# Slack behind DMA landings for scores and for VectorE and ScalarE steps in a recorded instruction order, and one store moved to another queue

## The chip, the cores and the metric

One core of one Trainium2 chip. The metric is the device time of one execution in microseconds (us).

A ratio "to before" is the mean time of one kernel's runs over the mean of the other's runs of the same rounds, on the same chip, with a 95% interval. It is not quite the ratio of the medians that are quoted beside it.

## The reference

Two layers, each an attention with a compressive memory (segments of 512 tokens, 32 heads of 20) and a feed-forward block, on 2048 tokens of width 640. Cut to what matters:

```python
for s in range(N):                       # N = 4 segments of L = 512
    logits = einsum('bhqd,bhkd->bhqk', qs, ks) * scale + mask
    p = softmax(logits, axis=-1)         # scores, exponentials
    a_dot = einsum('bhqk,bhkd->bhqd', p, vs)
    a_mem = einsum('bhld,bhde->bhle', phi(qs), M) / (phi(qs) @ z + 1e-06)
    o = g * a_mem + (1.0 - g) * a_dot
    M = M + einsum('bhld,bhle->bhde', phi(ks), vs)     # memory, for the next segment
    z = z + sum_l phi(ks)
x = x + o @ wo
x = x + relu(layernorm(x) @ w1) @ w2     # then the same two blocks once more
```

## The kernel before: what the change touches

The program is not written in the order in which it runs. Some forty generators each yield the operations of one job (scores, exponentials, division, feed-forward, stores). A list scheduler, at build time, keeps a predicted clock for each engine and a predicted time for every semaphore value. It picks one operation after another and appends it to that engine's list, and the chip then runs each list in that order. I call this scheduler the recorder.

The choice is made by a key, of which the first entry is the predicted start plus a penalty:

```python
# Sched.run, cut
if isinstance(st[2], Op):
    heads.append((st[0], n, st, self._alts(st[2]), st[2], self._late(st[2])))
elif isinstance(st[2], Either):                       # score steps
    both, lone = st[2].fn()
    if both is not None:
        heads.append((st[0], n, st, self._alts(both), both, 0.0))      # no penalty
...
key = (round(start + late), 0.5 if op.urgent else prio, self.rank[id(st[1])], n)
if best is None or key < best[0]:
    best = (key, st, end, start, k, op)
```

The penalty existed only for TensorE. From the event SOFT_FROM on, an operation whose input has only just become ready is ranked as if it started later, by 400 ns where the input comes from an engine and by 1000 ns where it is a DMA that has to land:

```python
SOFT, SOFT_DMA, SOFT_FROM = 400, 1000, ("sc",6,4,1)    # the original has a line each

def _late(self, op):
    late = 0.0
    if op.alts[0][0] == "pe" and SOFT_FROM in self.events:
        ...
        for t in waits:
            k = (id(t[0]), t[1])
            late = max(late, self.t[k] + SEM_NS + PE_MARGIN + (SOFT_DMA if k in self.landed else SOFT) - start)
    if not op.lag or self.mode != "full":
        return late
    ...
```

The penalty moves no predicted time. It only lets other work go first. The predicted landing of a transpose is made here:

```python
tk = yield dma("sp", slot_sem, 32768 * n, lambda e: e.dma_start_transpose(dst, src), waits,
               issue=max(1400.0, 140.0 * n), lat=2400.0, rate=270.0, holds=True)
```

The VectorE step that is the first one of the division, a reciprocal that waits for a transposed buffer, otk:

```python
w = yield Need("otk", m)              # the transpose's landing
...
tr = yield dve(192, 1, lambda e: e.reciprocal(
    rv, tt.ap.rearrange("p b (h e) -> p b h e", h=4)[:, :, :, DH]), w + rd.tks)
```

The softmax here doesn't subtract the row's maximum and nothing guards it: scores larger than these inputs give would overflow.

## Time and profile before

559.84 us in the median of three runs (558.67 to 560.89).

| from the page and the views | before |
|---|---|
| span of the profiled execution | 556.5 us |
| TensorE busy / VectorE busy / ScalarE busy | 545.8 / 416.2 / 405.5 us |
| TensorE idle from 105.9 to 478.0 us | 2.54 us |
| VectorE's waits for otk, all of the span | 4.2 us in 5 |
| changes of matmul kind after 105.9 us | 263 |

The event of SOFT_FROM falls at 105.9 us, at score matmul 224 of 1024. The prediction says 264 changes of kind; it counted to the end of the span, the table to the last scores. TensorE's timeline shows one of the six gaps (columns: start, length, what, and in brackets the idle time just before and what ended it):

```profile
145.85 0.39 PE L1177 MATMUL ps<-pad 20*128 20x512 bf16 x4
146.67 0.85 PE L658 MATMUL ps<-wo_r,oT 128*128 128x320 bf16 x5 [0.43 <-DVE x_sb L1393]
```

The score matmuls are followed by nothing for 0.43 us, and the release came from VectorE's residual add.

### The profile page before, as it was taken

What the parts mean: (1) busy time and instruction counts of PE and PEld (TensorE: products, weight loads), DVE (VectorE), ACT (ScalarE), POOL (GpSimd) and SP (SyncE); (2) the same over time, 40 slices, a digit from 0 to 9 for tenths busy, and PEclk for the clock granted to TensorE, in tenths of its full rate; (3) what the DMA queues carried; (4) which work ended last, traced back from release to release, by engine and by line L of the source; (5) the groups of instructions that cost most, each with busy time, mean ns of one, the idle gap of its engine ahead of it and who ended that gap; (6) DMA issues with size and microseconds to landing.
All of it is one profiled execution on the core that took longest, in us unless ns stands there. A gap on an engine that the chain in (4) does not pass through costs nothing.

```text
span 556.5 us, 18928 instructions
## 1 busy us (share of the span) xinstructions
PE 545.8 (98%) x8265; PEld 308.0 (55%) x8265; DVE 416.2 (75%) x1063; ACT 405.5 (73%) x514; POOL 192.1 (35%) x302
## 2 busy tenths in 40 slices
PE   8999999999999999999999999999999999999997
PEld 7554554455454555646456554465555654666756
DVE  5967889888899898897778988889965767335102
ACT  5699889899677887798788887887765787432140
POOL 5346344333444244343433443335411433201000
PEclk9999999999999999999999999999999999999999
DMA  8695899844584158274284424872427412333101
GB/s 271 142 231 160 206 192 220 228 60 88 97 172 92 21 105 185 49 113 77 58 203 83 91 45 114 155 122 21 67 59 175 105 44 30 85 83 62 40 2 51
DMA packets 130292, 61.32 MB, mean 110 GB/s; under 512 B 109090, under 2 KB 120098, under 8 KB 130210
## 3 DMA queue, kind: packets, MB, share of 16 engines
q1 hardware_dynamic: 129792, 59.62, 49.7%
q8 instruction: 65, 1.06, 0.8%
q10 hardware_dynamic: 418, 0.49, 0.3%
q14 instruction: 17, 0.14, 0.1%
HBM read 20.57 MB, written 12.85 MB: 60 GB/s over the span
## 4 chain that ended last, share of the span: by engine, by line
PE 83%; DVE 7%; DMA 5%; ACT 2%; SPq 2%; issue 1%; POOL 0%; ACTq 0%; POOLq 0%
PE ps L658 39%; PE ps L661 24%; PE ps L1177 8%; PE ps L1271 6%; DMA otk<-otu 3%; ACT PT L1239 2%; PE ps L1057 1%; PE ps L1114 1%; DMA pad<-scr 1%; PE ps L1310 1%; PE ps L635 1%; PE ps L1451 1%; DVE o_sb L1365 1%; DVE xn_tok L725 1%; SPq L993 1%; DMA scr<-w_r 1%
## 5 line engine op out<-in xcount | busy, mean ns | idle before, releaser
L1239 ACT ACTIVATE PT<-ps 128x1024 bf16<-128x1024 f32 x320 | 309.0, 1028 | 65.9 <-PE ps L1177 61.5
L1251 POOL TENSOR_SCALAR_AFFINE_SELECT PT<-PT 128x512 bf16<-128x512 bf16 x256 | 166.3, 668 | 265.4 <-ACT PT L1239 265.3
L658 PE MATMUL ps<-w_r,hT 128*128 128x320 bf16 x508 | 81.5, 299 | 0.0
L1497 DVE TENSOR_TENSOR x_sb<-x_sb,ps 128x320 bf16<-128x320 bf16 (+1 forms) x65 | 30.8, 474 | 55.3 <-PE ps L661 45.7
L661 PE MATMUL ps<-xnT,w_r 128*32 128x512 bf16 x1144 | 68.3, 379 | 0.3 <-issue 0.3
L1177 PE MATMUL ps<-pad 20*128 20x512 bf16 (+3 forms) x1024 | 63.4, 301 | 3.0 <-ACT PT L1239 2.1
L658 PEld LDWEIGHTS ps<-w_r,hT 128*128 128x128 bf16 x508 | 47.4, 98 | 23.6 <-issue 5.3
L679 DVE BATCH_NORM_STATS2 stats<-x_sb 128x6 f32<-128x320 bf16 x124 | 55.6, 470 | 2.9 <-DMA x_sb<-in_A_x_dram 2.5
L658 PE MATMUL ps<-xnT,w_r 128*128 128x512 bf16 x234 | 57.7, 380 | 0.0
L1476 ACT ACTIVATE hT<-ps 128x512 bf16<-128x512 f32 x57 | 34.1, 599 | 22.0 <-PE ps L661 20.7
L661 PE MATMUL ps<-w_r,hT 128*32 128x320 bf16 (+1 forms) x1348 | 49.7, 294 | 0.0
L1177 PEld LDWEIGHTS ps<-pad 20*128 20x128 bf16 x1024 | 17.9, 92 | 54.7 <-ACT PT L1239 24.5
L661 PEld LDWEIGHTS ps<-xnT,w_r 128*32 128x32 bf16 x1144 | 29.5, 97 | 24.8 <-issue 0.5
L1281 DVE CAST otu<-ps 128x512 bf16<-128x512 f32 x51 | 34.9, 684 | 10.9 <-PE ps L1271 10.8
L1271 PE MATMUL ps<-PT,v_aug 128*21 128x128 bf16 (+3 forms) x896 | 40.5, 301 | 0.0
L661 PEld LDWEIGHTS ps<-w_r,hT 128*32 128x32 bf16 x1348 | 34.6, 97 | 8.9
L1393 DVE TENSOR_TENSOR x_sb<-x_sb,ps 128x320 bf16<-128x320 bf16 x64 | 30.0, 477 | 11.8 <-PE ps L661 8.6
L1475 DVE TENSOR_SCALAR hT<-ps 128x512 bf16<-128x512 f32 x47 | 32.2, 685 | 7.2 <-PE ps L658 5.5
L695 POOL TENSOR_TENSOR rstd<-lnU,mhalf 128x2 f32<-128x2 f32 (+2 forms) x26 | 20.6, 792 | 45.1 <-DVE lnU L691 35.7
L658 PE MATMUL ps<-wo_r,oT 128*128 128x320 bf16 x223 | 35.4, 300 | 0.4 <-DVE x_sb L1393 0.4
L658 PEld LDWEIGHTS ps<-xnT,w_r 128*128 128x128 bf16 x234 | 20.9, 97 | 23.7 <-issue 4.3
L1022 ACT ACTIVATE stg<-stg 128x512 bf16<-128x512 bf16 x50 | 31.5, 634 | 2.5 <-DVE rtmp L1020 2.2
(109 smaller groups left out, 737.8 us busy)
## 6 DMA issues: line engine op xcount, KB each, us to landing
pad<-scr SPq DMA_DIRECT2D x124, 80.0 KB
scr<-stg SPq DMA_DIRECT2D x34, 256.0 KB, 3.5
out_dram<-x_sb SPq DMA_DIRECT2D x15, 160.0 KB, 1.8
w_r<-in_B_w_dram SPq DMA_DIRECT2D x10, 216.0 KB, 2.4
w_r<-in_B_w_dram SPq DMA_DIRECT2D x13, 160.0 KB, 2.9
x_sb<-in_A_x_dram SPq DMA_DIRECT2D x10, 160.0 KB, 3.2
scr<-w_r SPq DMA_DIRECT2D x5, 256.0 KB, 3.2
wv_r<-in_A_wv_dram SPq DMA_DIRECT2D x1, 800.0 KB, 9.0
```

Of the source, the lines that this page charges most:

```text
L658: return e.matmul(view(dst.ap, b), a, b, start=(k == 0), stop=(k == last))
L661: return e.matmul(view(dst.ap[rows], b), part, b, start=(k == 0), stop=(k == last))
L679: tk = yield dve(320, 1, lambda e, c2=c2: e.bn_stats(stats6[:, t % 12, c2, :], x_sb[:, t, c2 * 320:(c2 + 1) * 320]), xt)
L1022: te = yield act(512, lambda e, q=q: e.activation(q, q, ACT.Exp), [tr] + p, psum=False)
L1177: fns.append([(lambda e, z=z, j=j, hh=hh, N=N, o=o, sl=sl, q=hh % 2: e.matmul(slot.ap[:, q, o:o + N], sl.ap[32 * hh:32 * hh + DH, z, 0, 12 ...
L1239: tx = yield act(1024, lambda e, dst=dst, src=src: e.activation(dst, src, ACT.Exp, scale=SCALE), sc + pw)
L1251: tm = yield pool(600.0, lambda e, reg=reg: e.affine_select(out=reg, in_=reg, pattern=[[0, 4], [1, 128]], compare_op=ALU.is_ge, fill=0.0, ...
L1271: fns.append((lambda e, OD, j=j, hh=hh: e.matmul(OD.ap[32 * hh:32 * hh + DH + 1, 128 * j:L], VAUG[vx(a, s)][:, j, 4 * g + hh, :], pt.ap[:, ...
L1281: te = yield evac(L, 1, lambda e: e.tensor_copy(dst, OD.ap), lambda e: e.activation(dst, OD.ap, ACT.Copy), [tk] + OTU[0].tks)
L1475: th = yield evac(512, 1, lambda e: e.tensor_scalar(hT[:, dc, :], bk.ap[:, :], 0.0, None, ALU.max), lambda e: e.activation(hT[:, dc, :], b ...
L1476: lambda e: e.activation(hT[:, dc, :], bk.ap[:, :], ACT.Relu), [tk] + HT.tks)
L1497: ta = yield dve(n, 1, lambda e: e.tensor_tensor(x_sb[:, t, c0:c0 + n], x_sb[:, t, c0:c0 + n], bk.ap[:, 0:n], ALU.add), [tk], urgent=True)
```

## The change

The intent: landings come earlier or later than the recorder thinks, and each engine's list runs in order, so a step that waits for a landing should not stand at the head of a list just when the landing is due. The same slack that TensorE operations have is given to score steps and to steps of the other engines. The last quarter of the output is also issued from ScalarE's queue in place of SyncE's.

```diff
+    def _landing(self, op):
+        start = max([self.free["pe"]] + [self.at(t) + SEM_NS + PE_MARGIN for t in op.waits])
+        soft = SOFT_DMA if SOFT_FROM in self.events else 0.0
+        return max([0.0] + [self.at(t) + SEM_NS + PE_MARGIN + soft - start for t in op.waits
+                           if (id(t[0]), t[1]) in self.landed])
+
     def _late(self, op):
 ...
+        if op.alts[0][0] != "pe" and op.dma is None and SOFT_FROM in self.events:
+            start = max([self.free[op.alts[0][0]]] + [self.at(t) + SEM_NS for t in op.waits])
+            late = max([0.0] + [self.at(t) + SEM_NS + 1000 - start for t in op.waits if (id(t[0]), t[1]) in self.landed])
         if not op.lag or self.mode != "full":
             return late
 ...
-                        heads.append((st[0], n, st, self._alts(both), both, 0.0))
+                        heads.append((st[0], n, st, self._alts(both), both, self._landing(both)))
 ...
-                        S.last = yield dma("sp", dout, 256 * n, lambda e, c0=c0, n=n: e.dma_start(
+                        S.last = yield dma(("sp", "sp", "act")[hf], dout, 256 * n, lambda e, c0=c0, n=n: e.dma_start(
```

## The prediction

> **What bounds the kernel now.** I read the page first, then the busy time by stretch, then the waits of TensorE, and last the chain of waits around TensorE's few gaps. The first line of the page says which engine sets the time:
>
> ```profile
> span 556.5 us, 18928 instructions
> ...
> PE 545.8 (98%) x8265; PEld 308.0 (55%) x8265; DVE 416.2 (75%) x1063; ACT 405.5 (73%) x514; POOL 192.1 (35%) x302
> ```
>
> TensorE is busy for 545.8 us of 556.5, VectorE and ScalarE for three quarters. So an idle microsecond of VectorE or ScalarE costs nothing by itself; it costs only where TensorE then stands still. The program is recorded ahead of time by a list scheduler in the source: it picks the order of each engine's instructions from predicted times, and the chip runs each engine's list in that order. The change touches that order, and only after the event ("sc",6,4,1), the last scores of the seventh pair of head groups. A pair has 32 score matmuls (1024 for 32 pairs), so this is score matmul 224, which starts 105.9 us into the span. The other end is 478.3 us, the last score matmul. What TensorE does in the two stretches after that event:
>
> ```profile
> core 0: us, PE busy (x) PEld busy (x) DVE busy (x) ACT busy (x) POOL busy (x), PEclk, DMA share, GB/s
> 105.90:478.00 372.10, 369.56 (x5139) 200.15 (x5131) 308.65 (x774) 298.15 (x362) 142.77 (x217) 1.00 0.48 97
> 478.00:553.60 75.60, 75.55 (x1865) 50.98 (x1854) 22.33 (x55) 18.83 (x31) 3.06 (x5) 1.00 0.20 47
> ```
>
> Each line is length, then busy time by engine. Over the 372.10 us that the new order can change, TensorE is idle 372.10 - 369.56 = 2.54 us; over the last 75.60 us, 0.05 us. The granted clock is 1.00. The view of waits of TensorE over the same stretch names what ended those 2.5 us:
>
> ```profile
> PE ps L1177 <- ACT PT L1239: 1.3, 2, 0.7
> PE ps L1177 <- DMA pad<-scr: 0.5, 1, 0.5
> PE ps L658 <- DVE x_sb L1393: 0.4, 1, 0.4
> PE ps L658 <- DVE v_aug L912: 0.2, 1, 0.2
> ```
>
> Columns are us in total, times, longest. Only one wait is for a landing directly: scores (L1177) waiting 0.5 us for their pad buffer. The others are waits for ScalarE and VectorE, and the chain that ended last shows what stood behind them. Before the gap at 146.67 us, where the output projection waited for a residual add (x_sb L1393) to free its bank:
>
> ```profile
> 140.31 5.01 DMA otk<-otu
> 145.32 0.02 issue
> 145.34 0.35 DVE rden L1357
> 145.69 0.07 DVE mv L681
> 145.76 0.46 DVE rden L1360
> 146.22 0.79 DVE x_sb L1393 x2
> ```
>
> Columns are start, length, what. VectorE's own timeline shows the mechanism:
>
> ```profile
> 145.34 0.35 DVE L1357 RECIPROCAL rden<-otk 128x32 f32<-128x32 bf16 x1 [1.01 <-DMA otk<-otu]
> ```
>
> VectorE stood 1.01 us in front of a reciprocal whose transposed input had not landed; the scheduler had expected it about then. Everything recorded behind it, the residual adds too, came a microsecond late, and TensorE lost 0.43 us at 146.67 us. The same view for the whole kernel gives "DVE rden L1357 <- DMA otk<-otu: 4.2, 5, 1.0": five such waits, 4.2 us of VectorE. Another (1.04 us, at 189.7 us) stands at the head of the chain into the gap of 0.63 us at 194.9 us, and a third (0.68 us, at 415.3 us) at the head of the chain into the gap of 0.46 us before the last segment's first scores at 425.1 us. In that one the pad landing itself came last.
>
> **What the Trainium skill says.** "PSUM — Partial Sum Buffer", section "Engine vs sequencer instructions": the queues of ScalarE, VectorE and GpSimd are strictly first in, first out. The trace agrees: 1.01 us of idle VectorE at 144.3 us, then adds that did not need the landing. So the recording order alone decides whether a late landing blocks unrelated work. "TensorEngine Tiling (Array Packing)", section "Key Properties": changing the tiling mode drains TensorE. The trace agrees, and gives the price: a 512-column matmul over all 128 rows is followed after a median 216 ns by one of its own kind (439 pairs) but after 312 ns by a score matmul on 20 rows (48 pairs), so some 96 ns a change. I count 264 changes of kind after 105.9 us, 264 x 0.096 = 25 us. "DMA: Bandwidth & Descriptors", section "Issuing engines are not separate DMA queues": issuing from several engines runs on the same 16 DMA engines and saves only the sequencer's issue time. This matters for the last part of the change, below.
>
> **The change part by part.**
> No instruction is added or removed, apart from one store that moves to another queue. Up to 105.9 us the order should be the same: all three new terms are zero until the event is recorded.
>
> Scores. A score step whose pad landed less than 1 us ago (predicted) now yields to other TensorE work. It can concern only the first scores of a pair; 25 of the 32 pairs come after the event, and with four pad buffers most were loaded long before. The trace has one gap of this kind after 105.9 us: 0.46 to 0.53 us at 425.1 us. Worth up to 0.5 us if other work is there to fill it; at 422 to 425 us TensorE was already running output projection for lack of scores, so I count half, 0.25 us.
>
> VectorE and ScalarE. Any step that waits for a landing now ranks as if it could start 1 us after it. These are the reciprocals of the division (L1357), the feature-map steps that wait for the spill to memory (L1020, L1022), and the copies into a buffer which a transpose has just left (L1281). Idle VectorE time in front of landings after 105.9 us is 4.2 (transposes) + 0.5 (spills) = 4.7 us. I expect most of it to go, but VectorE has 308.65 of 372.10 us busy, so it is worth only the TensorE gaps behind it: 0.43 at 146.67 us, some 0.31 (hidden in the modelled ends, 310 ns over the usual start-to-start distance) at 151.8 us, 0.63 at 194.9 us: 1.4 us. The slack has a cost too: the division, and with it the transposes of o and the next loads, may be recorded up to 1 us later. I choose new gaps of 0.6 us in sum.
>
> Sum of gaps: -0.25 - 1.4 + 0.6 = -1.05 us. A floor: even all 2.5 us of gaps together are 0.45% of 559.84.
>
> Changes of kind. A new order also changes how often TensorE goes between score mode and the others. Nothing in the change aims at it; the four-column-group form of the projections lets the scheduler avoid some. I allow 15 changes more or fewer of 264, 15 x 0.096 = 1.4 us either way, with a mean of zero.
>
> The last quarter's store from ScalarE's queue. The group view of that store:
>
> ```profile
> L1525 SPq DMA_DIRECT2D out_dram<-x_sb x3: 332/333/1025, 552.2 to 553.9; - x3
> ```
>
> Three stores, durations minimum/median/maximum. The third starts at 553.95 us, right after its add ends (553.60 + 0.32 = 553.92), and the one before it started at 552.98 and took 0.33, so the queue was free 0.6 us earlier. There is no issue wait to remove. The odd 1025 ns of the third issue lies under its own flight: issue to landing was 2.1/2.2/2.9 us for the three, and the third took 2.2. With the same 16 DMA engines underneath, I expect -0.1 us, the chance of overtaking the slow second store.
>
> Together -1.05 - 0.1 = -1.15; with a little more weight on the good side, as the slack does remove the very waits seen, I take 558.4 us, that is 1.4 us or 0.26% off 559.84.
>
> **The rivals.**
> One: the order is hidden anyway. TensorE is at 369.56 of 372.10 us, and the gaps come back elsewhere because each is 0.3 to 0.7 us, the size of the scheduler's error. Then the result is 559.2 to 560.3, nothing to be seen beside the 558.67 to 560.89 of the three runs. For it: the gaps are few and each has another cause at its end. Against it: three of the four largest have a late landing in their chain.
> Two: changes of kind dominate. If pushed-back scores are grouped better with other four-group work, 20 to 30 fewer changes make -2 to -3 us, 556.5 to 557.5; if scores are split off more, +2 us, 561.5. Nothing in the profile tells which.
> Three: the slack starves the score pipeline at the segment starts. ScalarE already waits 56.5 us for scores after 105.9 us; six segment starts later by 1 us each would be 6 us if TensorE had nothing else. Against it: in the last 75.60 us TensorE runs only feed-forward work with 0.05 us idle, so late scores mostly exchange places with it. I would expect at most 2 us, 561 us.
>
> **Range and chances.** Gaps can give back at most 2.5 us, changes of kind some 1.4 us either way, the tail 0.3 us, and the median of few runs moves by about 1 us. From 558.4 this gives 555.8 to 560.9 for 8 in 10. Two per cent is 11.2 us, over four times the gaps there are; it would take over a hundred fewer changes of kind. So faster by over 2%: 0.02; slower by over 2%: 0.02, for a schedule that goes wrong at a segment start; within 2%: 0.96.
>
> **What would show it.** The new profile should show the same start of the score matmuls up to 105.9 us; TensorE idle of about 1.5 us between 105.9 us and the last scores in place of 2.54; VectorE waits for otk under 1.5 us in place of 4.2; changes of kind within 15 of 264; the third quarter's store issued by ScalarE, landing 2.1 to 2.3 us later. It would be wrong if TensorE's busy time itself moved by over 2 us (changes of kind), if new gaps of over 1 us stood at segment starts, or if the store from ScalarE's queue were issued late or flew longer.

## The result and the profile after

556.49 us in the median of four runs (556.20 to 557.13), against 560.37 us before (558.67 to 561.07). The ratio is 0.9937 with an interval of 0.9911 to 0.9962: 0.6% faster, within 2%. The predicted 558.4 us missed the median by 1.9 us; the range of 555.8 to 560.9 us holds it.

The page of the changed kernel:

```profile
span 554.8 us, 18665 instructions
...
PE 545.8 (98%) x8130; PEld 309.3 (56%) x8130; DVE 412.2 (74%) x1061; ACT 407.3 (73%) x516; POOL 190.0 (34%) x302
```

TensorE's busy time is the same to the tenth, 545.8 us; what went is idle time. The recorder itself had planned the changed order 0.45 us longer (TensorE's end at 547.99 us against 547.54): the plan got longer and the execution shorter. (The planned ends quoted in this document come from running the scheduler of each kernel, not from a trace.) (The counts of matmuls differ because some records are missing from each trace.) The same two stretches as in the prediction, their common end being the last score matmul, now at 476.4 us:

```profile
core 0: us, PE busy (x) PEld busy (x) DVE busy (x) ACT busy (x) POOL busy (x), PEclk, DMA share, GB/s
105.90:476.40 370.50, 369.38 (x5010) 200.93 (x5011) 306.60 (x776) 300.09 (x364) 141.19 (x217) 1.00 0.48 98
476.40:552.00 75.60, 75.26 (x1854) 50.86 (x1846) 22.25 (x55) 18.82 (x31) 2.78 (x5) 1.00 0.24 47
```

TensorE is idle 370.50 - 369.38 = 1.12 us in place of 2.54. The view of its waits over that time has two lines left in place of four:

```profile
PE ps L667 <- DVE hT L1484: 0.9, 1, 0.9
PE ps L1186 <- ACT PT L1248: 0.2, 1, 0.2
```

Line numbers are nine higher in the changed kernel (L1357 is now L1366, L1393 is L1402). At the place of the gap shown above there is none. VectorE's timeline there:

```profile
145.65 1.44 DVE L1402 TENSOR_TENSOR x_sb<-x_sb,ps 128x320 bf16<-128x320 bf16 x3 [0.77 <-PE ps L667]
147.31 0.35 DVE L1366 RECIPROCAL rden<-otk 128x32 f32<-128x32 bf16 x1 [0.22 <-DMA otk<-otu]
```

Three residual adds now run ahead of the reciprocal, which itself waits 0.22 us where it had waited 1.01. VectorE still idles 0.77 us, but in front of an add whose matmul was not done, and TensorE shows no gap there.

The one large gap that is left, 0.86 us at 107.4 us, has the old shape. The chain of waits into it:

```profile
99.72 5.55 DMA otk<-otu
105.27 0.02 issue
105.29 0.35 DVE rden L1366
...
106.73 0.61 DVE hT L1484
107.34 0.05 issue
107.39 0.82 PE ps L667 x3
```

A comparison of the two traces shows that VectorE's first 254 instructions, up to 115.8 us in the trace of before, are the same in both kernels, and TensorE's list up to score matmul 248. So at 107 us both kernels run the same order. The kernel before did not show this gap in its profile, and another run of the changed order (below) did not either. The transpose simply landed later in this execution.

This can be counted, and it is the cleanest evidence in the record. Twelve of the fourteen profiles in this document run the same order here (early_5 and compute_slack, below, do not). In all twelve this transpose of otk is issued 6.3 us before the score matmul of the event. In seven (before, dve_act_only, no_store, store_only, landing_early, all_but_divide, landing_late) it landed 4.26 to 5.04 us after its issue, VectorE waited at most 0.51 us for it, and TensorE shows no gap. In five (the change, scores_only, divide_only, slack_300, slack_2000) it took 5.40 to 5.85 us, VectorE waited 0.86 to 1.32 us, and TensorE then stood still for 0.68 to 0.86 us. The order is fixed, only the landing moves, and the gap comes and goes with it.

### The profile page after: what moved, and what is told of

Read it like the earlier page. It is cut to its first block, busy times and chain, and to the rows that moved or that the text cites. A ratio compares the mean times of both kernels' runs of the same rounds, so it can differ in the third digit from the quotient of the medians.

```text
span 554.8 us, 18665 instructions
## 1 busy us (share of the span) xinstructions
PE 545.8 (98%) x8130; PEld 309.3 (56%) x8130; DVE 412.2 (74%) x1061; ACT 407.3 (73%) x516; POOL 190.0 (34%) x302
## 3 DMA queue, kind: packets, MB, share of 16 engines
q8 instruction: 64, 1.05, 0.8%
## 4 chain that ended last, share of the span: by engine, by line
PE 93%; ACT 2%; DVE 2%; DMA 2%; SPq 0%; issue 0%; POOL 0%; ACTq 0%; POOLq 0%
PE ps L667 45%; PE ps L670 26%; PE ps L1186 9%; PE ps L1280 6%; ACT PT L1248 2%; PE ps L1319 1%; PE ps L1066 1%; PE ps L1123 1%; PE ps L644 1%; DMA otk<-otu 1%; PE ps L1460 1%; DMA beta_bc<-in_A_beta_dram 1%; SPq L982 0%; ACT stg L867 0%; PE ps L758 0%
## 5 line engine op out<-in xcount | busy, mean ns | idle before, releaser
L1260 POOL TENSOR_SCALAR_AFFINE_SELECT PT<-PT 128x512 bf16<-128x512 bf16 x256 | 164.2, 659 | 264.4 <-ACT PT L1248 264.3
L670 PE MATMUL ps<-xnT,w_r 128*32 128x512 bf16 x1112 | 65.4, 379 | 0.2 <-issue 0.2
L667 PE MATMUL ps<-xnT,w_r 128*128 128x512 bf16 x242 | 59.9, 380 | 0.9 <-DVE hT L1484 0.9
L1402 DVE TENSOR_TENSOR x_sb<-x_sb,ps 128x320 bf16<-128x320 bf16 x64 | 30.0, 479 | 18.2 <-PE ps L667 10.3
L667 PE MATMUL ps<-wo_r,oT 128*128 128x320 bf16 x242 | 38.9, 300 | 0.0
L1290 DVE CAST otu<-ps 128x512 bf16<-128x512 f32 x48 | 32.7, 682 | 6.9 <-PE ps L1280 6.3
L866 DVE CAST stg<-ps 128x512 bf16<-128x512 f32 x45 | 30.6, 684 | 5.8 <-PE ps L667 5.6
```

Of the source, the lines that this page charges most:

```text
L667: return e.matmul(view(dst.ap, b), a, b, start=(k == 0), stop=(k == last))
L670: return e.matmul(view(dst.ap[rows], b), part, b, start=(k == 0), stop=(k == last))
L866: te = yield evac(N, 1, lambda e: e.tensor_copy(sg.ap[:, t0:t0 + N], bk.ap[:, 0:N]), lambda e: e.activation(sg.ap[:, t0:t0 + N], bk.ap[:, ...
L1260: tm = yield pool(600.0, lambda e, reg=reg: e.affine_select(out=reg, in_=reg, pattern=[[0, 4], [1, 128]], compare_op=ALU.is_ge, fill=0.0, ...
L1290: te = yield evac(L, 1, lambda e: e.tensor_copy(dst, OD.ap), lambda e: e.activation(dst, OD.ap, ACT.Copy), [tk] + OTU[0].tks)
```

## The experiments

Twelve kernels ran, in three calls of four, each call on one chip with 11 runs of the kernel before beside it and 6 runs of each kernel (5 rounds and the profiled one). All gave correct results. "Idle" is TensorE's idle time from the event to the last score matmul in the profiled execution. "Event to end" is the time from the event to TensorE's last matmul in it; it leaves out what happened before the order differs.

| kernel | ratio to before | interval | median, us | idle, us | event to end, us |
|---|---|---|---|---|---|
| before (profile of the first runs) | 1 | | 560.37 | 2.54 | 447.7 |
| the change | 0.9937 | 0.9911 to 0.9962 | 556.49 | 1.12 | 445.7 |
| scores_only | 0.9991 | 0.9961 to 1.0021 | 558.93 | 1.72 | 448.1 |
| dve_act_only | 0.9959 | 0.9936 to 0.9981 | 557.38 | 0.68 | 445.9 |
| no_store | 0.9939 | 0.9916 to 0.9961 | 556.23 | 0.88 | 445.5 |
| store_only | 0.9995 | 0.9973 to 1.0017 | 559.51 | 3.27 | 448.7 |
| divide_only | 0.9960 | 0.9937 to 0.9982 | 557.49 | 1.75 | 447.1 |
| landing_early | 1.0078 | 1.0048 to 1.0108 | 563.74 | 5.79 | 453.2 |
| compute_slack | 0.9976 | 0.9950 to 1.0002 | 558.35 | 2.55 | 447.8 |
| slack_300 | 0.9974 | 0.9949 to 1.0000 | 558.20 | 1.55 | 446.3 |
| all_but_divide | 0.9977 | 0.9954 to 1.0000 | 557.59 | 0.89 | 446.5 |
| early_5 | 0.9964 | 0.9945 to 0.9984 | 556.92 | 1.01 | 445.6 |
| slack_2000 | 0.9997 | 0.9969 to 1.0025 | 559.15 | 2.14 | 447.5 |
| landing_late | 1.0100 | 1.0075 to 1.0126 | 564.46 | 7.34 | 454.1 |

The medians of before in the three calls were 559.68, 559.46 and 558.80 us, so compare by ratio and not by median across calls.

### The parts alone: scores_only, dve_act_only, no_store, store_only

My theory: the gain is TensorE gaps behind landings that block VectorE's list, so the slack on VectorE and ScalarE carries it. The rivals: the scores' placement carries it; the store does; any new order does.

scores_only: `_landing` and its use alone.

```diff
-                        heads.append((st[0], n, st, self._alts(both), both, 0.0))
+                        heads.append((st[0], n, st, self._alts(both), both, self._landing(both)))
```

> Only the scores' slack behind pad landings (the store stays on SyncE's queue). My theory, that the gain is TensorE gaps behind landings which block an in-order VectorE: this part removes at most the gap of 0.46 us at the last segment's first scores, ratio to before 0.998 to 1.001. Rival (the gain comes from scores that are placed better): ratio 0.995 or lower and most of the whole change's 0.9937. Rival (any new order is worth about this much): anything from 0.993 to 1.004.

Measured: 0.9991, not to be told from 1. TensorE's order is the same as before up to score matmul 788. The gap of 0.46 us at the last segment's first scores (425.1 us before) is gone, as was expected of this part. VectorE's waits for otk rose from 4.2 to 12.5 us, 6.2 us of them in one wait, and the time did not: here such waits cost nothing by themselves.

dve_act_only: the three lines in `_late` alone.

```diff
+        if op.alts[0][0] != "pe" and op.dma is None and SOFT_FROM in self.events:
+            start = ...
+            late = max([0.0] + [self.at(t) + SEM_NS + 1000 - start for t in op.waits if (id(t[0]), t[1]) in self.landed])
```

> Only the slack behind landings for VectorE, ScalarE and GpSimd steps. My theory: most of the gain is here, ratio to before 0.994 to 0.997, VectorE's waits for the transposed otk fall from 4.2 us to under 2.5 us, TensorE idle from the event to the last scores falls from 2.54 to under 1.5 us. Rival (scores are what counts): ratio 0.999 to 1.001.

Measured: 0.9959, idle 0.68 us, VectorE's waits for otk 0.4 us in all. This part gains by itself, and its point estimate is some two thirds of the whole.

no_store: both slack parts, the store as before.

```diff
-                        S.last = yield dma(("sp", "sp", "act")[hf], dout, 256 * n, ...
+                        S.last = yield dma("sp", dout, 256 * n, ...
```

> Both slack parts, last quarter's store still on SyncE's queue. My theory: the store is worth nothing (0.0 +- 0.2 us), so the ratio is the whole change's 0.9937 within 0.001. Rival (the store's queue counts): 0.995 or higher.

Measured: 0.9939, the whole gain. With 0.88 us idle and no gap near 107 us it is also a second look at the changed order. Against dve_act_only its mean is 1.0 us lower, give or take about as much, so on top of the other slack the scores' slack may be worth more than it is alone. Part of this may be changes of kind: dve_act_only has about five more, some 0.5 us at the prediction's 96 ns each (an estimate).

store_only: the one line of the store alone, on the kernel before.

```diff
-                        S.last = yield dma("sp", dout, 256 * n, ...
+                        S.last = yield dma(("sp", "sp", "act")[hf], dout, 256 * n, ...
```

> Only the last quarter's store on ScalarE's queue; the order of TensorE, VectorE and GpSimd is the same as before instruction by instruction. My theory: ratio 0.9995 to 1.0005, the third store issues 0.03 us after its add as before and lands 2.1 to 2.3 us later. Rival: it issues or lands 0.3 us or more earlier, ratio 0.999 or lower.

Measured: 0.9995. The lists of TensorE, VectorE and GpSimd are the same as before, row by row. The store's group view:

```profile
L1525 SPq DMA_DIRECT2D out_dram<-x_sb x2: 332/332/332, 554.0 to 554.8; - x2
L1525 ACTq DMA_DIRECT2D out_dram<-x_sb x1: 368/368/368, 555.8 to 555.8; - x1
```

The third store took 368 ns to issue from ScalarE's queue. From SyncE's it had taken 1025 ns in the profile of before, but its data flew 2.19 us then and 2.31 us here. Nor is 1025 ns the price of SyncE's queue: the same store took 332 or 333 ns from it in scores_only, divide_only, compute_slack and all_but_divide, each time with a flight of 1.5 us. The time that ends the span is the flight. Over the profiled executions it was either near 2.2 us or near 1.5 us from either queue: 1.50 us from SyncE's in divide_only, 1.53 us from ScalarE's in early_5. The move is worth nothing that these runs can see.

This run is also a second look at the order of before, and here lies the size that the prediction missed. The order is the same, the idle time is 3.27 us and not 2.54. TensorE's timeline has a gap which the first profile did not have at all:

```profile
165.06 0.30 PE L658 MATMUL ps<-w_r,hR 128*128 128x320 bf16 x1
166.07 1.89 PE L658 MATMUL ps<-xnT,w_r 128*128 128x512 bf16 x8 [0.71 <-DMA xnT<-xn_tok]
```

In the profile of before the matmuls of the same place ran back to back (164.24 and 164.37 us). I compared the 86 transposes of the two executions one by one, from issue to landing: they differ by 0.16 us on the mean, seven by more than 0.5 us, and the largest difference is 0.98 us. So the same list meets landings that move by up to a microsecond, and which gap opens changes from run to run.

### Which step, and is it the landing: divide_only, all_but_divide, landing_early, compute_slack

divide_only: the slack applies to the division's first reciprocal alone. (In this and the next control the diff is shown against the change's line; the edit was made on the kernel before, without the scores' slack and the store, and also marks the reciprocal with `divides`.)

```diff
-        if op.alts[0][0] != "pe" and op.dma is None and SOFT_FROM in self.events:
+        if getattr(op, "divides", False) and SOFT_FROM in self.events:
```

> Slack of 1 us for one step of VectorE only: the reciprocal that waits for the transposed otk (28 of them). My theory, that late transposes in front of this in-order reciprocal are the main cause: ratio to before 0.994 to 0.997, as with the slack on all VectorE and ScalarE steps (0.9959), VectorE's waits for otk under 1 us. Rival (feature-map steps and copies count as much): ratio 0.998 or higher.

Measured: 0.9960, the same as the slack on every VectorE, ScalarE and GpSimd step. VectorE's waits for otk fell to 1.3 us, not under the 1 us that was expected, but all of it lies before the event.

all_but_divide: every such step but that one.

```diff
-        if op.alts[0][0] != "pe" and op.dma is None and SOFT_FROM in self.events:
+        if op.alts[0][0] != "pe" and op.dma is None and SOFT_FROM in self.events and not getattr(op, "divides", False):
```

> Slack of 1 us for VectorE, ScalarE and GpSimd steps behind landings, but not for the division's reciprocal. My theory: the reciprocal carries the gain, so this is worth nothing, ratio to before 0.998 to 1.001, VectorE's waits for otk 3 us or more. Rival (any one of the parts moves the order to the better): 0.997 or lower.

Measured: 0.9977, with waits for otk of 6.7 us. The expectation of 0.998 or more missed narrowly, and the interval of 0.9954 to 1.0000 reaches both to divide_only's value and to nothing. So divide_only shows that slack on the reciprocal is enough for about two thirds of the gain (by the point estimates); that the rest of the steps are worth nothing is not shown. The profiles do not separate the two kernels either: all_but_divide idles 0.89 us and takes 446.5 us from event to end, divide_only 1.75 and 447.1 us.

The recorder's own model separates them clearly. I replayed each recorded list with the model's durations and let every transpose from the event on land 1 us later than planned. TensorE's end then moves from 547.54 to 559.00 us for before, from 547.58 to 558.51 us for all_but_divide, but only from 548.56 to 549.69 us for divide_only and from 547.99 to 549.59 us for the change. This is the plan and not the chip, where landings move by less and not all together. It shows what the slack buys: an order that late transposes hardly lengthen, and slack on the one reciprocal is enough for that.

landing_early: no slack, but a recorder that expects transposes 1 us earlier from the event on.

```diff
-                           issue=max(1400.0, 140.0 * n), lat=2400.0, rate=270.0, holds=True)
+                           issue=max(1400.0, 140.0 * n), lat=1400.0 if SOFT_FROM in S.events else 2400.0, rate=270.0, holds=True)
```

> No slack anywhere; instead the recorder believes, from the same event on, that every transpose lands 1 us earlier than before. This doubles the suspected cost. My theory: VectorE's waits for otk grow from 4.2 us to 12 us or more, more TensorE gaps stand behind them, ratio to before 1.004 or higher. Rival (the gain of the change is luck of a new order): ratio anywhere from 0.994 to 1.004 with no relation to the waits.

Measured: 1.0078. The recorder's own predicted end of TensorE hardly moved (547.77 us against 547.54), but that is a plan in which transposes land 1 us earlier. Replayed with the landings that before's recorder expects, the same order ends at 559.13 us, so by plan it is 11.6 us worse. On the chip VectorE's waits for otk grew to 15.1 us in 13, TensorE's idle time to 5.79 us. The largest gap shows all links at once; first VectorE's line, then TensorE's two, both from the timeline of landing_early:

```profile
419.86 0.35 DVE L1357 RECIPROCAL rden<-otk 128x32 f32<-128x32 bf16 x1 [2.94 <-DMA otk<-otu]
```

```profile
431.98 0.31 PE L661 MATMUL ps<-w_r,hT 128*32 128x320 bf16 x4
435.22 0.60 PE L1177 MATMUL ps<-pad 20*128 20x512 bf16 x4 [2.94 <-DMA pad<-scr]
```

VectorE stood 2.94 us before the reciprocal. The feature maps recorded behind it came late, the next pads were issued late, and TensorE found nothing to do for 2.94 us at 432.3 us. The chain of waits of this run goes from the one to the other without a break; its two ends, with 33 pieces between them left out:

```profile
415.20 4.64 DMA otk<-otu
419.84 0.02 issue
419.86 0.37 DVE rden L1357
...
431.28 3.90 DMA pad<-scr
435.18 0.05 issue
435.22 0.60 PE ps L1177 x4
```

So the largest gap stands where the theory puts it, in a list made tighter behind transposes. The ratio alone is no proof: landing_late (below), which makes nothing tighter, is slower still. And it is not a clean doubling. The edit moves all transposes, and 1.9 us of the idle time are TensorE's own waits for oT, which slack on VectorE would not touch. After the gap of 2.94 us the granted clock was one half for 3.41 us, an extra 1.7 us (an estimate: half of the stretch).

compute_slack: a control. The same lines, for waits that are not landings:

```diff
-            late = max([0.0] + [... + 1000 - start for t in op.waits if (id(t[0]), t[1]) in self.landed])
+            late = max([0.0] + [... + 400 - start for t in op.waits if (id(t[0]), t[1]) not in self.landed])
```

> Control: the same kind of slack (400 ns) for VectorE, ScalarE and GpSimd steps that wait for other engines' work, none for landings. It gives another order in which landings are as tight as before. My theory: ratio 0.998 to 1.003, VectorE's waits for otk 3 us or more. Rival (any new order with slack gains): ratio 0.996 or lower.

Measured: 0.9976, an interval just reaching 1. The expected lower end of 0.998 was missed by a little, and the miss is instructive. VectorE waited 8.8 us for otk, twice as much as before, and the kernel was no slower. TensorE's idle time is 2.55 us, as before. So VectorE's waiting is no measure by itself; what TensorE lacks behind it is. In the replay with transposes 1 us late this order is as tight as before, as it was meant to be (547.41 to 558.50 us). And part of what looks like gain, up to the 0.24% of this control, may be the luck of another order.

### How much slack: slack_300, slack_2000, early_5, landing_late

slack_300 and slack_2000: the whole change with another size (300 here; 2000 in the other).

```diff
-            late = max([0.0] + [self.at(t) + SEM_NS + 1000 - start for t in op.waits ...
+            late = max([0.0] + [self.at(t) + SEM_NS + 300 - start for t in op.waits ...
```

> The whole change with 300 ns in place of 1000 ns for VectorE and ScalarE steps. The waits for landings seen are mostly 0.7 to 1.3 us late, so 300 ns should cover few of them. My theory: VectorE's waits for otk above 2.5 us, ratio to before 0.995 to 0.999, between scores alone and the whole change. Rival (the size does not matter, only that the order differs): 0.9937 as with 1000 ns.

> The whole change with 2000 ns in place of 1000 ns for VectorE and ScalarE steps. My theory: landings are covered already at 1000 ns, so nothing more is gained and the division and its loads come later: VectorE's waits for otk below 1.5 us, ratio to before 0.994 to 0.998. Rival (more slack removes more gaps): 0.992 or lower.

Measured: 0.9974 and 0.9997. With 300 ns VectorE's waits for otk stay at 5.6 us, as predicted; with 2000 ns they are 2.1 us where under 1.5 was expected, and the ratio misses the 0.994 to 0.998 that was expected. But here the profiles give a warning. In both profiled executions the score matmul of the event came at 108.6 and 109.0 us, 2 to 3 us later than in most others, although the lists are the same as before up to there. The timeline and the stretches of slack_300 (columns of the second as above) say why:

```profile
37.10 0.56 PE L1123 MATMUL ps<-w_r,phk 128*128 128x147 bf16 x6 [1.05 <-DVE o_sb L1336]
```

```profile
32.00:36.00 4.00, 3.68 (x63) 2.02 (x60) 1.50 (x4) 3.29 (x6) 1.86 (x3) 1.00 0.99 211
36.00:40.00 4.00, 2.94 (x27) 1.85 (x25) 1.97 (x5) 2.93 (x4) 1.22 (x2) 0.74 0.98 218
40.00:44.00 4.00, 3.97 (x47) 1.82 (x47) 1.82 (x4) 2.85 (x3) 1.91 (x3) 0.83 0.65 210
```

A gap of 1.05 us opened at 36.1 us, and from 37.9 us on the granted clock was one half for 3.41 us. The same happened in slack_2000 after a gap of 1.10 us. It is not the slack's doing, and one such event costs some half of 3.41 us, 1.7 us, on top of the gap (an estimate): about half of the effect under study. The six times of slack_2000 (560.72, 556.49, 556.99, 560.77, 559.44, 558.87) lie in no narrow cluster, and its profiled execution is the second slowest. The granted clock is on record for each run, and a stretch of 3.41 us at half clock lowers its mean by 0.003: three of the six (560.72, 560.77, 559.44) have 0.997, the others 1.000. Without the runs under 0.999, of either kernel, the ratio of the plain means is 0.9976 for slack_2000 (three runs left) and 0.9978 for slack_300 (five left), too few to tell them from each other or from the change. So the ratio of slack_2000 is diluted by such events, and the one that its profile shows lies before the slack begins; that 300 ns is too little, or 2000 ns too much, is not settled.

early_5: the whole change, but the VectorE and ScalarE slack starts one pair of head groups earlier.

```diff
+SOFT_V = ("sc",5,4,1)
-        if op.alts[0][0] != "pe" and op.dma is None and SOFT_FROM in self.events:
+        if op.alts[0][0] != "pe" and op.dma is None and SOFT_V in self.events:
```

> The whole change, its VectorE and ScalarE slack beginning one pair of head groups earlier (near 95 us in place of 106 us), because four profiles with reordering have a TensorE gap of 0.7 to 1.0 us near 107 us behind a transpose that landed at 105.3 us and was recorded just before the event. My theory: that gap goes, ratio to before 0.992 to 0.994, at or a little below the whole change's 0.9937. Rival (other gaps take its place): 0.994 to 0.997.

Measured: 0.9964. The gap at 107 us is absent, but the order there is another one and the transpose took only 4.34 us, so the absence says nothing. Small gaps of 0.3 to 0.4 us stand at 130.7, 139.4 and 237.4 us, and event to end is 445.6 us, as with the change. The rival named in the expectation fits better. The reason given there was also wrong: at 107 us the change had not yet altered anything, and no_store had no gap there. No version beat the changed kernel.

landing_late: no slack, but a recorder that expects transposes 1 us later from the event on.

```diff
-                           issue=max(1400.0, 140.0 * n), lat=2400.0, rate=270.0, holds=True)
+                           issue=max(1400.0, 140.0 * n), lat=3400.0 if SOFT_FROM in S.events else 2400.0, rate=270.0, holds=True)
```

> No slack; the recorder believes from the event on that each transpose lands 1 us later. Rank and belief both move. My theory: VectorE's waits for otk go to under 1.5 us as with the slack, but everything that depends on a transpose is also planned 1 us later at each segment start, so that the gain is eaten up: ratio to before 0.997 to 1.004. Rival (a late belief is as good as slack): 0.993 to 0.996.

Measured: 1.0100, worse than even the pessimistic theory. Waits for otk did not fall under 1.5 us but stayed at 4.7 us, and TensorE idled 7.34 us. The profiled execution includes a stretch of half clock of 6.83 us at 168.0 us, after gaps of 1.06 and 0.80 us; the event-to-end time of 454.1 us contains some 3.4 us for it (an estimate: half of the stretch). All six runs have a mean granted clock of 0.990 to 0.994, so by the same estimate 3.4 to 5.6 us of each run's time are half clock, most of the 5.7 us that this kernel loses. The plan itself was worse: the recorder put TensorE's end at 552.94 us, 5.4 us later than before. Believing every landing late delays all that depends on it, in the plan and on the chip. Slack only changes who goes first.

## Why the prediction was right or wrong, point by point

- **The bound, and where the gain can come from: right.** TensorE's busy time stayed at 545.8 us; the gain is TensorE idle time, 2.54 to 1.12 us in the profiles.
- **The mechanism (a late transpose at the head of VectorE's list): right, and shown.** In twelve profiles of one order the gap at 107 us is there in the five with a landing of 5.40 us or more and in none of the seven with 5.04 us or less. Slack on that one reciprocal gives 0.9960, and in landing_early the chain from the reciprocal's wait to TensorE's largest gap is in one piece. How much of the 0.63% is this and how much is the luck of another order is not shown (rival two, below).
- **"Sum of gaps: -0.25 - 1.4 + 0.6 = -1.05 us": right against the profile, too small against the medians.** Profile against profile, the span fell by 556.5 - 554.8 = 1.7 us, close to the 1.4 us forecast. The medians fell by 3.9 us. The mis-sized term is the 2.54 us of gaps that the whole sum starts from. It was read off an execution of 558.5 us, 1.9 us under the median, and taken for the kernel. A second execution of the same order had 3.27 us idle and came 1.0 us later from event to end (448.7 against 447.7). Two executions of the changed order took 445.7 and 445.5 us, so the pair differs by 448.2 - 445.6 = 2.6 us on the mean.
- **The floor, "even all 2.5 us of gaps together are 0.45%": wrong as a floor.** It held for one execution only. The idle time also leaves out part of each loss: the matmul at 151.8 us started 310 ns later than its kind does, with 145 ns shown as idle; the one at 425.1 us 527 ns with 459 ns. Over the six gaps this is some 0.6 us, an estimate from those start-to-start distances. And a gap of a microsecond was followed by 3.41 us at half clock in slack_300 and slack_2000. The record shows such executions of before too: of its 33 runs beside the experiments six have a mean granted clock of 0.993 to 0.997, the longest, 562.46 us, with 0.993. They are not the main part of the miss: with all runs under 0.999 left out, the ratio of the plain means is still 0.9945 for no_store and 0.9963 for dve_act_only.
- **Changes of kind, mean zero: right.** 263 before, 264 after, counted between the same two score matmuls.
- **Scores, half of 0.5 us: right for the part alone, within what can be seen.** scores_only is 0.9991 +- 0.003, and the gap it aimed at is gone. On top of the other slack it came out at 1.0 us (no_store against dve_act_only), where 0.5 us was named as the most, but six runs of each can't tell that from nothing.
- **The store, -0.1 us: right that it is nothing.** 0.9995 +- 0.002 alone; the third store lands 2.28 us after its issue, within the 2.1 to 2.3 us named.
- **VectorE's waits for otk under 1.5 us: missed as said, 2.5 us.** Of these 1.03 us lie at 105.3 us, before the order changes; from the event on they are 1.5 us.
- **Rival one (gaps come back elsewhere) and rival three (starved segment starts):** new gaps in the changed order were 0.08 and 0.18 us in its profile, and up to 0.49 us at a segment start (356.7 us) in no_store. Neither rival decides.
- **Rival two (luck of the order) stays partly open.** Its carrier, changes of kind, did not move. But compute_slack, which aims at no landing, has 0.9976, and its interval ends at 1.0002. Its 0.24% is more than a third of the measured 0.63%, and these runs can't tell that share from luck. In the replay compute_slack tolerates late transposes no better than before, so if its gain is real it has another cause.

The Trainium skill was used for three facts in the prediction, and the runs agree with the first two. For "DMA: Bandwidth & Descriptors", section "Issuing engines are not separate DMA queues", store_only fits as well: the store from the other queue flew 2.31 us against 2.19, and the time did not move. A saving of issue time is not shown, as SyncE's issue took 333 ns in other runs.

## What to carry to other kernels

In a list that is recorded from predicted times, rank work behind a DMA landing a little later than its predicted time, so that unrelated work on the same in-order engine goes first; do not push the prediction itself. Look at what the bound engine loses behind such waits, not at how long the waiting engine waits. And where a change is worth less than 1%, take a second profile of the unchanged kernel before sizing it: two executions of one order differed here by 1.0 us after the event alone, against a forecast of 1.4 us in all. And where several profiles share an order up to some point, compare them there first: what differs between them is the landings and not the order.

## What the Trainium skill lacked or had wrong

- "TensorE: Matmul & The Clock Gate", section "HAM oscillation — how this bites in real kernels", gives the rule that no idle gap should exceed about 3.4 us. Here shorter gaps came before a half-clock stretch: 1.05 us (slack_300) and 1.10 us (slack_2000), each followed by 3.41 us at half clock, and gaps of 1.06 and 0.80 us (landing_late), followed by 6.83 us. Not every such gap does it: 2.35 us at 371.2 us in landing_late, 1.30 us at 308.3 us in landing_early and 1.02 us at 108.3 us in compute_slack were followed by full clock. The next section of that page does say that frequent micro-idling makes the gate oscillate, for another kernel. The length of 3.41 us agrees with the window that the page's section "What's actually happening" states.
- No page gives the spread of a DMA transpose's landing between executions. Here 86 transposes, in two executions of the order of before, differed by 0.16 us on the mean and by 0.98 us at most; in two of the changed order by 0.22 and 1.51 us.
- I found no page that tells of two levels of a store's flight ("DMA: Bandwidth & Descriptors", section "Anatomy of one DMA — SWDGE (gpsimd) path", states a fixed cost of about 2.0 us for the path from GpSimd, and section "Latency and other measured facts" that it is smaller under lighter HBM load). The last 40 KB store took about 2.2 us or about 1.5 us from issue to landing in different executions, from either queue.
